# First batch row: Prelus, exponentials and conversion steps put ahead of the turns, and the second turn copy of every unit on ScalarE

## The chip, the core and the metric

The kernel runs on one core of one Trainium2 chip. A core has five engines, each with an instruction stream of its own: TensorE (PE, matmuls and transposes through it), VectorE (DVE), ScalarE (ACT), GpSimd (POOL) and SyncE (SP, which here issues DMA transfers). They meet at semaphores. Matmul results land in PSUM[...].

The metric is device microseconds of one execution. Before the change three runs gave 1376.87, 1380.67 and 1382.66 us; the median is **1380.67 us**. The profiled execution has a span of 1375.1 us, and all times within the span below are counted from its start.

## What is computed

Attention in which only the scores near the row's maximum survive, and then an MLP mixer over tokens and channels. All data are float32; the four MLP weights arrive as float64, and the kernel itself turns them into float32.

```python
# q, k, v: (8 batches, 8 heads, 576 tokens, 64)
scores = q @ k.transpose(0, 1, 3, 2) / 8
thresh = scores.max(-1, keepdims=True) - tau
scores = np.where(scores >= thresh, scores, -1e9)
attn   = np.exp(scores - scores.max(-1, keepdims=True))
attn   = attn / (attn.sum(-1, keepdims=True) + 1e-9)
x      = (attn @ v) as (8, 576, 512)

h   = np.maximum(x.transpose(0, 2, 1) @ w_tok1, 0) @ w_tok2     # over tokens
u   = x + h.transpose(0, 2, 1)
out = u + np.maximum(u @ w_ch1, 0) @ w_ch2                      # over channels
```

## The kernel before

The work of a batch row is cut into 18 units: two pairs of head pairs, nine units each; a unit is 128 query tokens of two heads, which are called h = 0 and 1. Units 0 to 17 are batch row 0. In this row no MLP work is there yet to fill gaps, and the exponentials are transposed by TensorE, through PSUM; this is a "turn". In later rows VectorE and DMA transpose them, and MLP steps are filled in between. The weights are converted from float64 from the start on, in small steps, three to a piece; 31 pieces in all.

The order in which the code emits instructions is the order in which each engine gets its own. The loop, for the first row:

```python
for u in range(len(units) + LAG + 4):            # LAG = 2
    ...
    w = u - LAG
    if on:
        scores(u)
    last = False
    if due and not in_blocks(due[0][1]):
        last = values_due(u)                     # values matmuls, after every third turn
    if 0 < u <= len(units):
        norm(u - 1)
    if b_now:
        weight(2)
    else:
        weight_to(2.25 * (u - 1.5))              # conversion steps, first part
    while copies:
        copies.popleft()()                       # xT <- pv, VectorE (L420)
    ...
    if back:
        wb, wp, wt = units[w]
        if not in_blocks(wb):
            for i in range(3):
                turn(w, i)                       # the turns of the unit two back
        ...
    if b_now:
        weight(2)
    if on:
        weigh(u)                                 # Prelus and exponentials
    ...
    if b_now:
        weight(2)
    elif u == 0:
        ...
    else:
        weight_to(2.25 * (u - 1))                # conversion steps, second part
    ...
        if t == 2:
            prep(n + 1)                          # q, k transposes on VectorE (L284)
        if t == 7 and n + 2 < len(pairs):
            prep(n + 2)
```

What a unit does, with the line numbers that the profile uses:

```python
def scores(u):
    sc = [(ps_3rd if b == 0 and (2 * u + h) % 3 == 2 else ps_sc).tile([P, 2, MAIN], ...) for h in range(2)]
    ...
        nc.tensor.matmul(sc[h][rows, f, 0:HS], lhsT=qT[r, cols], rhs=kT[...], ...)          # L302
    for h in range(2):
        nc.vector.tensor_reduce(out=mx[:, c], in_=sc[h][:, :, 0:HS], op=ALU.max, ...)       # L307
        nc.gpsimd.tensor_scalar(out=bias[:, c], in0=mx[:, c], scalar1=toff, ...)            # L308

def weigh(u):
    for h in range(2):
        nc.scalar.activation(out=eh, in_=sc[h][:, :, 0:HS], func=AF.Prelu, bias=..., ...)   # L317
    ...
    for h in range(2):
        nc.scalar.activation(out=eh, in_=eh, func=AF.Exp, accum_out=rs[:, h : h + 1], ...)  # L324

def norm(u):
    nc.vector.tensor_scalar(out=rr, in0=rs, ...)                                            # L331
    nc.vector.reciprocal(out=rr, in_=rr)                                                    # L332
    for h in range(2):
        nc.gpsimd.tensor_scalar(out=eh, in0=eh, scalar1=rr[:, h : h + 1], ...)              # L335

def turn(u, third):
    ...
    ps = ps_tr.tile([P, MAIN], F32, tag="tr", ...)          # two buffers, shared with the values matmuls
    for c in range(3):
        nc.tensor.transpose(out=ps[:, c, :], in_=e[:, k0 : k0 + P], identity=ident)         # L353
    on = nc.scalar.copy if third == 1 and u % 2 else nc.vector.tensor_copy
    on(out=eTs[key][...], in_=ps)                                                           # L355
```

`turn` is called with u two units back, so the ScalarE copies of odd units fall into odd units of the loop. The score tiles of the first row have three buffers, two to a unit: with the first Prelu of a unit the buffer comes free that the next unit's second score tile needs.

A conversion step k belongs to piece k // 3; each emits one VectorE instruction and, by its part, GpSimd's last instruction of the piece before with the load of a later piece, or one ScalarE instruction of the next piece:

```python
def weight(n):
    for k in range(steps_done, min(steps_done + n, 3 * len(pieces) + 1)):
        i, part = divmod(k, 3)
        if part == 0:
            on_gpsimd(i - 1)                     # L215
            if i:
                load_piece(i - 1 + NRAW)         # NRAW = 4 raw buffers
        else:
            on_scalar(i + 1, part - 1)           # L191, L193
        on_vector(i, part)                       # L201, L205, L209
        steps_done = k + 1

def weight_to(x):
    weight(max(int(x) - steps_done, 0))
```

Of the kernel before, what the change touches and what calls it, by code (L numbers as in the profile page):

```python
# [21 lines left out]
def kernel(  # L22
# [25 lines left out]
    nc = tc.nc  # L48
# [174 lines left out]
    def weight(n):  # L223

        nonlocal steps_done
# [5 lines that stand above are left out]
                    load_piece(i - 1 + NRAW)  # L231
            else:
                on_scalar(i + 1, part - 1)
            on_vector(i, part)
# [5 lines that stand above are left out]
# [36 lines left out]
    def in_blocks(b):  # L276
        return b > 0
# [10 lines left out]
    def scores(u):  # L288
        b, p0, t = units[u]
        sc = [  # L290
            (ps_3rd if b == 0 and (2 * u + h) % 3 == 2 else ps_sc).tile([P, 2, MAIN], F32, tag="sc", name=f"sc{h}_{u}") for h in range(2)
        ]
        if t == SHARED:
            parts = [(b * NP + p0, slice(MAIN, S), slice(0, 64)), (b * NP + p0 + 1, slice(0, LAST), slice(64, P))]
        else:
            o = P * t if t < SHARED else LAST + P * (t - SHARED - 1)
            parts = [(b * NP + p0 + (t > SHARED), slice(o, o + P), slice(0, P))]
        order = [(f, part, h) for f in range(2) for part in parts for h in range(2)]
        for f, (n, cols, rows), h in order if b else sorted(order, key=lambda o: o[2]):
            r = slice(D * h, D * h + D)  # L300
            qT, kT = heads[n]
            nc.tensor.matmul(sc[h][rows, f, 0:HS], lhsT=qT[r, cols], rhs=kT[r, HS * f : HS * f + HS], start=True, stop=True)  # L302
        mx = small.tile([P, 2], F32, tag="mx", name=f"mx_{u}")
        bias = small.tile([P, 2], F32, tag="bias", name=f"bias_{u}")
        for h in range(2):
            c = slice(h, h + 1)
            nc.vector.tensor_reduce(out=mx[:, c], in_=sc[h][:, :, 0:HS], axis=AX.XY, op=ALU.max)  # L307
            nc.gpsimd.tensor_scalar(out=bias[:, c], in0=mx[:, c], scalar1=toff, scalar2=-SCALE, op0=ALU.add, op1=ALU.mult)  # L308
        st[u] = sc, bias

    def weigh(u):
        sc, bias = st.pop(u)
        rs = small.tile([P, 2], F32, tag="rs", name=f"rs_{u}")
        e = work.tile([P, 2 * S], F32, tag="e", bufs=3, name=f"e_{u}")
        for h in range(2):
            eh = e[:, S * h : S * h + S].rearrange("p (f x) -> p f x", f=2)
            nc.scalar.activation(out=eh, in_=sc[h][:, :, 0:HS], func=AF.Prelu, bias=bias[:, h : h + 1], scale=SCALE, alpha=STEEP)  # L317
        st[u] = e, rs

        if b_now:  # L320
            fill(0.2)
        for h in range(2):
            eh = e[:, S * h : S * h + S]
            nc.scalar.activation(out=eh, in_=eh, func=AF.Exp, bias=ntau, accum_out=rs[:, h : h + 1])  # L324
            if b_now:
                fill(0.2)

    def norm(u):
        e, rs = st[u]
        rr = small.tile([P, 2], F32, tag="rr", name=f"rr_{u}")  # L330
        nc.vector.tensor_scalar(out=rr, in0=rs, scalar1=1e-9, scalar2=None, op0=ALU.add)  # L331
        nc.vector.reciprocal(out=rr, in_=rr)  # L332
        for h in range(2):
            eh = e[:, S * h : S * h + S]
            nc.gpsimd.tensor_scalar(out=eh, in0=eh, scalar1=rr[:, h : h + 1], scalar2=1.0, op0=ALU.mult, op1=ALU.mult)  # L335
        st[u] = e
# [3 lines left out]
    def turn(u, third):  # L340

        b, p0, t = units[u]
        key, place = (b, p0, t // GU), t % GU
        e = st[u]

        if third == 0 and place == 0:
            eTs[key] = work.tile([P, NK, GU * P], F32, tag="T", name=f"eT_{u}")
        if third == 2:
            st.pop(u)
        ps = ps_tr.tile([P, MAIN], F32, tag="tr", name=f"tr{third}_{u}")[:, 0 : 3 * P].rearrange("p (c x) -> p c x", c=3)  # L350
        for c in range(3):
            k0 = (3 * third + c) * P
            nc.tensor.transpose(out=ps[:, c, :], in_=e[:, k0 : k0 + P], identity=ident)  # L353
        on = nc.scalar.copy if third == 1 and u % 2 else nc.vector.tensor_copy
        on(out=eTs[key][:, 3 * third : 3 * third + 3, P * place : P * place + P], in_=ps)  # L355

    def turn_blocks(u):
# [149 lines left out]
    def fill(share):  # L507
        nonlocal credit
        credit += share * quota
        while todo and credit > 0:  # L510
            cost, step = todo.popleft()
            credit -= cost
            step()
        if not todo:
            credit = 0.0

    def push(b):
        nonlocal quota
        uT = xTs[b]
        steps, old = token_mlp(b), list(todo)  # L520
        todo.clear()

        for i, step in enumerate(steps):
            n = 2 if i in (NT, NT + NTK) else 1
            todo.extend(old[:n] + [step])
            del old[:n]
        todo.extend(old)
        for i in range(2) if b % 2 == 0 else range(2, (2 * S + GR - 1) // GR):
            todo.extend(channel_mlp(b - b % 2, uT, i))
        quota = (sum(c for c, _ in todo) - (KEEP if b else KEEP_FIRST)) / (UB - 1)  # L530
# [3 lines left out]
    b_now = 0  # L534
    LAG = 2

    def values_due(u):
        while due and due[0][0] <= u:
            _, b, p0, g = due.popleft()
            values(b, p0, g)  # L540
            if p0 == NP - 2 and g == 2:
                if not in_blocks(b):
                    return True
                push(b)
        return False

    for u in range(len(units) + LAG + 4):
        on = u < len(units)
        if u == UB:
            late.close()  # L550
            ps_mm = ctx.enter_context(tc.tile_pool(name="ps_mm", bufs=2, space=bass.MemoryType.PSUM))
        if on:
            b_now, p0, t = units[u]
            n = b_now * NP + p0
        w = u - LAG
        back = 0 <= w < len(units)
# [5 lines that stand above are left out]
            last = values_due(u)  # L562
# [3 lines that stand above are left out]
            weight(2)  # L566
        else:

            weight_to(2.25 * (u - 1.5))
        while copies:  # L570
            copies.popleft()()
        if last:
            push(0)
# [4 lines that stand above are left out]
                    turn(w, i)  # L578
            if wt % GU == GU - 1:
                g = wt // GU  # L580
                if g < 2:
                    split_middle(wb * NP + wp + g)
                due.append((u + (2 if in_blocks(wb) else 1), wb, wp, g))
        if b_now:
            fill(0.4)
        if back and in_blocks(wb):
            turn_blocks(w)
        if b_now:
            weight(2)
        if on:  # L590
            weigh(u)
        elif b_now:
            fill(0.6)
        if b_now:
            weight(2)
        elif u == 0:
            on_scalar(0, 0)
            on_scalar(0, 1)
        else:
            weight_to(2.25 * (u - 1))  # L600
        if on:


            when = {3: (2, 0, 2), 4: (2, 2, 4), 5: (2, 4, 6), 6: (2, 6, 8), 8: (3, 0, 3), 0: (1, 3, 6), 1: (1, 6, 8)}
            if u == 0:
                load_qk(1, (nc.sync, nc.sync), range(0, 3))
            if t in when:
                m, lo, hi = when[t]
                if n + m < len(pairs):
                    load_qk(n + m, (nc.scalar if b_now else nc.sync,) * 2, range(lo, hi))  # L610
            if t in (3, 7) and n + 2 + t // 4 < len(pairs):
                load_v(n + 2 + t // 4)
            if t == 2:
                prep(n + 1)
            if t == 7 and n + 2 < len(pairs):
                prep(n + 2)
        if due and in_blocks(due[0][1]):
            values_due(u)
# [31 lines left out]
```

## Time and profile before

| engine | busy, us | share of the span | instructions |
|---|---|---|---|
| TensorE (PE) | 1322.7 | 96% | 6226 |
| VectorE (DVE) | 588.2 | 43% | 1017 |
| ScalarE (ACT) | 581.8 | 42% | 1288 |
| GpSimd (POOL) | 356.0 | 26% | 683 |

A row of the timeline reads: start in us, duration in us, engine, source line, operation, output tile <- input tiles, shapes, how many instructions are merged in the row, and in brackets how long the engine stood idle before it and what ended that wait. "q" behind an engine's name is its instruction queue, PEld the weight loads of TensorE. L302 is line 302 of the kernel. A row of the waits reads: who waited <- for whom: total us, times, longest us. In the table of slices each digit is the busy share of one fortieth of the span in tenths (9 is 90% or more), and PEclk the clock that TensorE was granted, in tenths of full speed.

### The profile page before, as it was taken

The numbers are of one execution on the slowest core, as the hardware profiler recorded it, in microseconds if no ns is written. First come the engines' busy times: TensorE is split into PE (matmuls) and PEld (weight loads), VectorE is DVE, ScalarE is ACT, GpSimd is POOL, SyncE is SP. The second block draws the span as 40 slices with busy tenths as digits, with TensorE's granted clock in tenths as the row PEclk, the third lists the DMA queues.
The fourth block names the chain that finished last, engine by engine and source line by source line (L and its number), as shares of the span: only waits on it lengthen the run. The fifth ranks groups of instructions, "written<-read, shape, count | busy, mean of one in ns | idle before, by whom it ended". The sixth has DMA issues, their size and how long they took to land.

```text
span 1375.1 us, 17691 instructions
## 1 busy us (share of the span) xinstructions
PE 1322.7 (96%) x6226; PEld 817.9 (59%) x6226; DVE 588.2 (43%) x1017; ACT 581.8 (42%) x1288; POOL 356.0 (26%) x683
## 2 busy tenths in 40 slices
PE   6877799999999999999999999999999999999998
PEld 3444465646565666565665567565656576575675
DVE  6788875445444443434244444434333453201000
ACT  5666654454445444443434444353333444120110
POOL 4555653222222222222122222222121222100000
PEclk9988999999999999999999999999999999999999
DMA  5434655454544354433344435434433442400000
GB/s 121 98 96 125 183 142 124 100 123 98 122 109 114 82 121 94 113 88 95 77 100 94 113 77 123 106 83 98 103 87 75 107 103 63 115 1 16 8 11 21
DMA packets 278871, 128.20 MB, mean 93 GB/s; under 512 B 200896, under 2 KB 271552, under 8 KB 278784
## 3 DMA queue, kind: packets, MB, share of 16 engines
q1 hardware_dynamic: 150176, 111.06, 32.0%
q10 hardware_dynamic: 128608, 16.01, 7.3%
q8 instruction: 50, 0.82, 0.3%
q14 instruction: 37, 0.30, 0.1%
HBM read 43.25 MB, written 9.44 MB: 38 GB/s over the span
## 4 chain that ended last, share of the span: by engine, by line
PE 85%; DVE 7%; DMA 2%; SPq 2%; ACT 1%; issue 1%; POOL 1%; ACTq 0%; DVEq 0%; POOLq 0%
PE c L486 26%; PE c L470 26%; PE sc L302 11%; PE pv L413 9%; PE t L441 5%; PE t L448 3%; PE pv L408 3%; DVE mx L307 2%; SPq L374 2%; PE tx L432 1%; PE c L482 1%; DMA eT<-T 1%; PE tr L353 1%; DVE wc L205 1%; ACT e L317 1%
## 5 line engine op out<-in xcount | busy, mean ns | idle before, releaser
L307 DVE TENSOR_REDUCE mx<-sc 128x1 f32<-128x576 f32 x288 | 204.5, 751 | 487.9 <-PE sc L302 487.5
L470 PE MATMUL c<-xT,wc 128*128 128x256 f32 (+1 forms) x1920 | 399.4, 362 | 2.1 <-DVE xT L452 1.2
L486 PE MATMUL c<-wc,g 128*128 128x512 f32 x864 | 390.5, 597 | 0.0
L470 PEld LDWEIGHTS c<-xT,wc 128*128 128x128 f32 x1920 | 334.5, 191 | 71.5 <-issue 27.6
L308 POOL TENSOR_SCALAR bias<-mx,toff 128x1 f32<-128x1 f32 x288 | 82.8, 288 | 799.3 <-DVE mx L307 742.3
L317 ACT ACTIVATE e<-sc,bias 128x576 f32<-128x576 f32 x288 | 199.6, 739 | 162.0 <-POOL bias L308 161.4
L486 PEld LDWEIGHTS c<-wc,g 128*128 128x128 f32 x864 | 157.8, 190 | 175.7 <-issue 174.0
L471 ACT ACTIVATE g<-c 128x256 f32<-128x256 f32 (+1 forms) x240 | 86.7, 362 | 334.1 <-PE c L470 317.9
L324 ACT ACTIVATE e<-e,ntau 128x576 f32<-128x576 f32 x288 | 220.7, 771 | 0.0
L335 POOL TENSOR_SCALAR e<-e,rr 128x576 f32<-128x576 f32 x288 | 215.6, 761 | 15.8 <-DVE rr L332 4.3
L302 PE MATMUL sc<-kT,qT 64*128 64x288 f32 (+1 forms) x1280 | 196.6, 447 | 11.1 <-DVE kT L284 7.1
L365 DVE STREAM_TRANSPOSE T<-e 128x1152 f32<-128x1152 f32 x126 | 172.1, 1366 | 6.3 <-DMA eT<-T 2.6
L302 PEld LDWEIGHTS sc<-kT,qT 64*128 64x128 f32 (+1 forms) x1280 | 107.4, 184 | 98.3 <-issue 59.1
L413 PE MATMUL pv<-eT,lv 128*64 128x384 f32 (+1 forms) x1024 | 136.8, 409 | 0.0
L413 PEld LDWEIGHTS pv<-eT,lv 128*64 128x64 f32 x1024 | 76.1, 138 | 51.0 <-issue 43.6
L491 DVE COPY o<-c 128x512 f32<-128x512 f32 x36 | 24.9, 692 | 177.5 <-PE c L486 177.5
L418 ACT COPY xT<-pv 128x384 f32<-128x384 f32 (+1 forms) x56 | 21.0, 401 | 157.5 <-PE pv L413 157.5
L448 PE MATMUL t<-w,a 128*128 128x288 f32 x256 | 75.2, 421 | 7.2 <-DVE xT L452 5.3
L441 PE MATMUL t<-x_sb,w 128*128 128x512 f32 x160 | 72.1, 598 | 0.0
L448 PEld LDWEIGHTS t<-w,a 128*128 128x128 f32 x256 | 45.6, 191 | 32.2 <-issue 11.4
L452 DVE TENSOR_TENSOR xT<-xT,t 128x288 f32<-128x288 f32 x64 | 28.2, 446 | 80.5 <-PE t L448 80.0
L324 ACT ACTIVATION_READ_ACCUMULATOR e<-e,ntau 128x1 f32 x288 | 56.5, 196 | 0.0
(44 smaller groups left out, 554.7 us busy)
## 6 DMA issues: line engine op xcount, KB each, us to landing
eT<-T SPq DMA_DIRECT2D x672, 108.0 KB, 2.2
scratch<-in_moe_w_ch_dram SPq DMA_DIRECT2D x24, 512.0 KB, 3.7
lv<-in_v_dram SPq DMA_DIRECT2D x32, 288.0 KB, 3.3
out_dram<-o SPq DMA_DIRECT2D x36, 256.0 KB, 2.2
lk<-in_k_dram ACTq DMA_DIRECT2D x111, 72.0 KB, 2.6
lq<-in_q_dram ACTq DMA_DIRECT2D x106, 72.0 KB, 2.3
lq<-in_q_dram SPq DMA_DIRECT2D x22, 72.0 KB, 3.2
lk<-in_k_dram SPq DMA_DIRECT2D x17, 72.0 KB, 3.3
```

The costliest lines, as they stand in the source:

```text
L302: nc.tensor.matmul(sc[h][rows, f, 0:HS], lhsT=qT[r, cols], rhs=kT[r, HS * f : HS * f + HS], start=True, stop=True)
L307: nc.vector.tensor_reduce(out=mx[:, c], in_=sc[h][:, :, 0:HS], axis=AX.XY, op=ALU.max)
L317: nc.scalar.activation(out=eh, in_=sc[h][:, :, 0:HS], func=AF.Prelu, bias=bias[:, h : h + 1], scale=SCALE, alpha=STEEP)
L324: nc.scalar.activation(out=eh, in_=eh, func=AF.Exp, bias=ntau, accum_out=rs[:, h : h + 1])
L335: nc.gpsimd.tensor_scalar(out=eh, in0=eh, scalar1=rr[:, h : h + 1], scalar2=1.0, op0=ALU.mult, op1=ALU.mult)
L365: nc.vector.transpose(out=T[:, :, place, :].rearrange("p a (c x) -> p c a x", c=NK), in_=e.rearrange("p (c a x) -> p c a x", c=NK, a=4))
L413: nc.tensor.matmul(to[r], lhsT=lv[:, j, :], rhs=e[j], start=False, stop=(c == NI - 1), skip_group_check=True)
L441: nc.tensor.matmul(ps, lhsT=w1[:, t, P * m : P * m + P], rhs=x_sb[:, t, :], start=(t == 0), stop=(t == NT - 1))
L448: nc.tensor.matmul(ps, lhsT=s["a"][:, m, P * c : P * c + P], rhs=w2[:, m, HS * f : HS * f + HS], start=(m == 0), stop=(m == NTK - 1))
L470: nc.tensor.matmul(ps, lhsT=wc1[:, j, c, :], rhs=uT[:, c, GR * i : GR * i + n], start=(c == 0), stop=(c == NCC - 1))
L471: nc.scalar.activation(out=s["g"][:, j, 0:n], in_=ps, func=AF.Relu)
L486: nc.tensor.matmul(flat, lhsT=s["g"][:, j, P * t : P * t + P], rhs=wc2[:, j, :], start=False, stop=(j == NJ - 1), skip_group_check=True)
```

## The change

Three things change, all of them for the first batch row. The second part of each turn is copied by ScalarE in every unit, not in odd ones alone, which takes work from VectorE. `weigh` is emitted ahead of the turns, so that ScalarE comes to a unit's Prelus and exponentials before it comes to a copy of a turn. And the two calls of `weight_to` become one, ahead of the turns, with as many steps at the unit's end as before.

```diff
@@ def turn(u, third)
-        on = nc.scalar.copy if third == 1 and u % 2 else nc.vector.tensor_copy
+        on = nc.scalar.copy if third == 1 else nc.vector.tensor_copy
@@ the loop over units, ahead of the copies and turns
-            weight_to(2.25 * (u - 1.5))
+            weight_to(2.25 * (u - 1))
+
+            if on:
+                weigh(u)
         while copies:
             copies.popleft()()
@@ behind the turns
-        if on:
+        if on and b_now:
             weigh(u)
         elif b_now:
             fill(0.6)
@@
         elif u == 0:
             on_scalar(0, 0)
             on_scalar(0, 1)
-        else:
-            weight_to(2.25 * (u - 1))
```

## The prediction

> **What bounds the kernel now.** I began with the page's table of slices (34.4 us each), to see where the one changed stretch lies.
>
> ```profile
> PE   6877799999999999999999999999999999999998
> ...
> DVE  6788875445444443434244444434333453201000
> ...
> PEclk9988999999999999999999999999999999999999
> ```
>
> From the sixth slice on TensorE is busy throughout at full clock, so what an earlier stretch gains or loses moves the end one for one. Only in the first four slices is VectorE (DVE) as busy as TensorE. The changed code acts on the first batch row, units 0 to 17, and its turns run on into units 18 and 19. Taking the start of a unit's first maximum (L307) as the unit's start, the timeline gives units 3 to 18 at 22.85, 26.78, 31.67, 39.70, 44.02, 48.98, 53.85, 58.45, 63.53, 71.48, 76.56, 82.27, 89.17, 93.14, 99.81 and 106.18 us. Those are 15 units in 83.3 us: 10 without values matmuls take 49.2 us (4.92 each), and 5 with them (5, 8, 11, 14, 17) take 34.1 us.
>
> Next, the timeline of unit 6, whose three turn copies are all on VectorE (rows of other engines left out):
>
> ```profile
> 39.70 1.42 DVE L307 TENSOR_REDUCE mx<-sc 128x1 f32<-128x576 f32 x2 [0.22 <-issue]
> ...
> 41.32 0.29 DVE L201 TENSOR_SCALAR w<-scratch 128x288 uint32<-128x288 uint32 x1
> ...
> 41.52 1.01 DVE L355 COPY eT<-tr 128x384 f32<-128x384 f32 x2
> ...
> 42.12 0.55 PE L353 MATMUL tr<-ident,e 128*128 128x128 f32 x3 [1.32 <-DVE eT L355]
> ...
> 42.60 1.25 PE L302 MATMUL sc<-kT,qT 64*128 64x288 f32 x8
> ...
> 42.71 0.56 DVE L355 COPY eT<-tr 128x384 f32<-128x384 f32 x1 [0.17 <-PE tr L353]
> ...
> 43.18 0.92 DVE L205 SCALAR_TENSOR_TENSOR w<-scratch,w 128x288 uint32<-128x288 uint32 x1
> ...
> 44.02 1.41 DVE L307 TENSOR_REDUCE mx<-sc 128x1 f32<-128x576 f32 x2
> ```
>
> There is a loop through two engines. TensorE does a unit's first two turn groups at once, but the third must wait until VectorE has copied one of them out (two "tr" buffers), and the next unit's scores stand behind that third group. VectorE hardly idles: while TensorE does the third group and the scores, it copies the second and third group and does one more conversion step (L205).
>
> In odd units ScalarE copies the second group. Unit 9:
>
> ```profile
> 54.60 0.48 ACT L355 COPY eT<-tr 128x384 f32<-128x384 f32 x1 [0.92 <-PE tr L353]
> ...
> 55.13 0.55 PE L353 MATMUL tr<-ident,e 128*128 128x128 f32 x3 [0.57 <-ACT eT L355]
> ```
>
> Here the third group goes 0.54 us before VectorE copies its first (55.67): it takes the buffer that ScalarE has freed, and waits for VectorE not at all.
>
> Last, the waits over 0 to 210 us (total, times, longest):
>
> ```profile
> ACT eT L355 <- PE tr L353: 23.2, 7, 6.1
> ...
> PE tr L353 <- DVE eT L355: 17.7, 8, 3.6
> ...
> DVE xT L420 <- PE pv L413: 7.7, 4, 2.9
> ```
>
> ScalarE stands 23.2 us before its turn copies, with the Prelus queued behind them. That looks like the thing to mend, but ScalarE is busy only 12 to 17 us of each 20 there.
>
> [...]in unit 5 ScalarE is idle 6.11 us before its copy at 37.60 and only then starts the Prelu at 37.97. So emission order matters.[...] the granted clock was 0.52 at 75 to 80 us and 0.66 at 95 to 100, and six transposes took 1.54 us where 0.88 is usual.[...] L205 on 288 columns took 0.92 us at 43.18, beside GpSimd's L215 at 43.05; 64x256 took 0.42 at 38.54 alone.
>
> **The change part by part.**
>
> 1. Nine copies of the second group (units 2, 4, ... 18) go from VectorE to ScalarE. Each adds about 0.5 us start to start on VectorE: 9 × 0.5 = 4.5 us of VectorE time. ScalarE gets 9 × 0.48 us, beside other work.
>
> 2. Prelus and exponentials go ahead of the turns. A Prelu no longer waits for a turn copy. The gain is where it held the next scores: the eight matmuls of unit 6, behind unit 5's late Prelu, took 2.05 us instead of 1.25. The price is that the ScalarE copy now comes after the exponentials. Counted from the unit's first maximum: maxima and the second bias 2.0, second Prelu 0.7, exponentials 1.6, so the copy runs from about 4.3 to 4.8. The build's waits show the consequence: the third group of every unit up to 15 now waits for VectorE, also in odd units.
>
> 3. All conversion steps (2 or 3 a unit) come ahead of the copies. They no longer lie under TensorE's third group and scores, but on the loop. From the rows above the loop becomes: two maxima and the reciprocal 1.61 (58.45 to L201 at 60.06 in unit 10); the steps W; first copy to third group 0.60 (41.52 to 42.12); third group to scores 0.48; scores to the next maximum 1.34 (52.51 to 53.85, where the maximum waited for the scores). That is 4.03 us + W. A step costs start to start 0.20 (L201), 0.40 (L205), 0.36 (L209) at 288 columns, and 0.35, 0.60, 0.60 at 512. From the start of the first copy VectorE then has 2.42 us until the next maximum and only two copies to do in it, the second from 1.19 to 1.74: about 0.7 us idle on either side of it.
>
> The steps that each unit gets, by the built order, give W; I add 0.2 us a unit for GpSimd's lock (the blocked steps of before lost some 4.4 us in 18 units). Unit 12 gets 0.45 more, for 16 short score matmuls (1.8 us). The q and k transposes in 7 and 16 (1.42 us) find 0.7 us idle and add 0.75.
>
> Units 3, 4, 6, 7, 9, 10, 12, 13, 15, 16 were 3.93, 4.89, 4.32, 4.96, 4.60, 5.08, 5.08, 5.71, 3.97, 6.67, sum 49.2. With W of 0.95, 1.2, 0.6, 0.56, 0.96, 0.6, 1.2, 1.55, 0.95, 1.2 they become 5.2, 5.4, 4.8, 5.5, 5.2, 4.8, 5.9, 5.8, 5.2, 6.2, sum 54.0 at full clock. Two of the ten at half clock, 1.0 us each for the longer third group and scores, make 56.0: **6.8 us lost**. The 4.5 us of part 1 is already inside this: it shortens VectorE's work, which no longer sets the loop.
>
> Units with values: TensorE's 3.7 to 4.7 us of pv set these, before and after, and the conversions lie under that wait (xT waited 2.85 us in unit 5). Unit 5 gains 1.0 (early Prelu, no step between the last copy and the maximum), 11 gains 0.25, 14 gains 0.55, 17 gains 0.7; unit 8, where pv was early and two steps now precede the xT copy, loses 0.3: **2.2 us won**. Unit 18's copy on ScalarE: 0.4 won. Units 0 to 2: nothing.
>
> Sum: +6.8 − 2.2 − 0.4 = +4.2 us, 1380.7 → 1384.9.
>
> **The rivals.** (a) VectorE's work is the bound, as its 96 to 99% in 25-30, 40-50 and 90-95 us suggests. Then the nine copies and shorter lock conflicts (4.5 + about 2) come off, with the 2.2 and 0.4: some 9 us, 1372. Against it: its filler is what moves. (b) ScalarE becomes the bound: conversions 0.9, Prelus 1.35, exponentials 1.6, copy 0.48 make 4.3 us a unit, below 4.9; but where its late copy still holds a buffer (the first group of the next unit waits for it, as built), a slip would add 0.5 us to some units: 1387. (c) Clock: if TensorE's wait for the first copy, now about 1.9 us in every unit instead of 1.3 to 3.0 in even ones,[...] three half-clock units fewer save 3 to 4 us, and it comes out even at 1380; if less often, 1388.
>
> **Range and chances.** The table rests on differences of tenths of a microsecond, and (a) and (c) both pull down, so I take 1383.0. Three runs of before differ by 5.8 us, as much as the effect: 1374 to 1391 should hold it 8 times in 10. A change of 2% is 27.6 us, nearly a third of the 83 us, and nothing here is so large: faster 0.015, same 0.97, slower 0.015.
>
> **What would show it.** Right: VectorE idle 0.5 to 0.7 us before the third-group copy and before the maximum in nearly every unit without values; ScalarE's wait before its copies far below 23.2 us; units of 4.8 to 6.2 us without values and 6.4 with; unit 18 starting about 4 us later than 106.18, and the rest shifted by that. Wrong: unit 18 starting at 98 to 102 us, the maxima of the next unit ready before VectorE is, or, against the one-for-one shift, a first row and an end that move by different amounts because the weight transfers of 140 to 195 us run at their own pace.

## The result and the profile after

The changed kernel takes **1390.32 us** in the median of six runs (1387.92 to 1394.34); the kernel before, run beside it, takes 1381.87 us (1376.87 to 1382.66). The ratio is **1.0069, with a 95% interval of 1.0048 to 1.0091**: some 9.5 us longer by this ratio (the two medians are 8.5 us apart). The time lies just inside the range that I gave. The size of the loss does not fit: I predicted 1383.0, a loss of 2 us, where the working itself had come to 4.2.

The table of slices of the changed kernel:

```profile
PE   5777799999999999999999999999999999999998
...
DVE  5668885454444444434333444433443453201000
...
PEclk7887999999999999999999999999999999999999
```

Only the first four slices differ in kind: TensorE and VectorE are both less busy, and the clock that TensorE is granted there is lower. Unit 18 starts at 119.43 us instead of 106.18, and from there to the end the two kernels stay 11.8 to 13.5 us apart: nothing is won or lost later. (Spans are 1387.1 and 1375.1 us. The runs of before, with those beside the experiments, spread from 1376.9 to 1386.5 us, and the profiled one took 1376.9, so the two traces are further apart than the medians.)

From here on, the **row length** is the time from the first maximum of unit 3 to that of unit 18; it leaves out the start of the span, after which unit 3 begins anywhere from 22.76 to 25.02 us from run to run. Busy times over just this stretch, before (us from start to end of the stretch: its length, then busy time and instructions of TensorE, its weight loads, VectorE, ScalarE and GpSimd, granted clock, DMA share, GB/s):

```profile
22.85:106.18 83.33, 66.54 (x411) 40.10 (x409) 68.34 (x146) 54.91 (x115) 48.74 (x79) 0.90 0.39 92
```

and after:

```profile
23.52:119.43 95.91, 69.48 (x413) 40.63 (x414) 64.12 (x138) 61.76 (x128) 53.69 (x79) 0.82 0.34 79
```

VectorE was indeed relieved (68.3 to 64.1 us), but the stretch is 12.6 us longer, so VectorE idles 31.8 us of it instead of 15.0. TensorE has the same work and takes 3 us more for it (69.5 for 66.5), at a granted clock of 0.82 for 0.90.

What it now waits for shows in the timeline of unit 9, an odd one, in the changed kernel:

```profile
60.38 1.42 DVE L307 TENSOR_REDUCE mx<-sc 128x1 f32<-128x576 f32 x2 [0.68 <-PE sc L302]
...
62.00 0.29 DVE L201 TENSOR_SCALAR w<-scratch 128x288 uint32<-128x288 uint32 x1
...
62.32 0.47 DVE L205 SCALAR_TENSOR_TENSOR w<-scratch,w 128x288 uint32<-128x288 uint32 x1
62.83 0.80 DVE L209 SCALAR_TENSOR_TENSOR w<-h,w 128x288 f32<-128x288 f32 x1
...
63.55 0.55 DVE L355 COPY eT<-tr 128x384 f32<-128x384 f32 x1
...
64.15 0.55 PE L353 MATMUL tr<-ident,e 128*128 128x128 f32 x3 [3.05 <-DVE eT L355]
...
64.52 0.46 ACT L355 COPY eT<-tr 128x384 f32<-128x384 f32 x1
...
64.63 1.57 PE L302 MATMUL sc<-kT,qT 64*128 64x288 f32 x8
64.73 0.56 DVE L355 COPY eT<-tr 128x384 f32<-128x384 f32 x1 [0.64 <-PE tr L353]
...
66.28 0.76 DVE L307 TENSOR_REDUCE mx<-sc 128x1 f32<-128x576 f32 x1 [0.99 <-PE sc L302]
```

Before, ScalarE copied this unit's second group out of PSUM 0.75 us after the first maximum began (54.60 against 53.85), and TensorE's third group followed at 1.28 us. Now ScalarE comes to the copy at 4.14 us, behind the Prelus and exponentials; the third group waits for VectorE's first copy, behind three conversion steps, and starts at 3.77 us. TensorE has stood still for 3.05 us by then, and its scores take 1.57 us where 1.25 is the quick value. VectorE idles 0.64 us before the third group's copy and 0.99 us before the next maximum.

The waits over the same stretch, after:

```profile
ACT e L317 <- POOL bias L308: 28.6, 23, 3.5
...
PE tr L353 <- DVE eT L355: 25.1, 10, 3.6
DVE mx L307 <- PE sc L302: 13.4, 14, 1.7
DVE eT L355 <- PE tr L353: 11.3, 15, 1.0
...
ACT eT L355 <- PE tr L353: 5.4, 4, 1.8
```

Before these were 5.2, 11.4, 1.7, 4.0 and 23.2 us. ScalarE's wait before its copies, which the change set out to mend, is down to 5.4 us; it now waits for the biases of the next unit instead (28.6 us). TensorE and VectorE wait for each other.

### The profile page after: what moved, and what is told of

It reads as the page before. It is cut to its first block, busy times and chain, and to the rows that moved or that the text cites. A ratio compares the mean times of both kernels' runs of the same rounds, so it can differ in the third digit from the quotient of the medians.

```text
span 1387.1 us, 17688 instructions
## 1 busy us (share of the span) xinstructions
PE 1324.0 (95%) x6226; PEld 815.9 (59%) x6226; DVE 584.1 (42%) x1008; ACT 587.2 (42%) x1297; POOL 361.7 (26%) x683
## 4 chain that ended last, share of the span: by engine, by line
PE 88%; DVE 6%; DMA 2%; SPq 1%; ACT 1%; issue 1%; ACTq 0%; POOL 0%; DVEq 0%; POOLq 0%
PE c L486 27%; PE c L470 26%; PE sc L302 12%; PE pv L413 9%; PE t L441 5%; PE t L448 3%; PE pv L408 3%; DVE mx L307 2%; SPq L374 1%; PE tx L432 1%; PE c L482 1%; PE tr L353 1%; DVE wc L205 1%; DMA eT<-T 1%; DVE wc L209 1%
## 5 line engine op out<-in xcount | busy, mean ns | idle before, releaser
L335 POOL TENSOR_SCALAR e<-e,rr 128x576 f32<-128x576 f32 x288 | 222.5, 785 | 15.7 <-DVE rr L332 4.6
L302 PEld LDWEIGHTS sc<-kT,qT 64*128 64x128 f32 (+1 forms) x1280 | 104.6, 183 | 100.1 <-issue 60.6
L448 PEld LDWEIGHTS t<-w,a 128*128 128x128 f32 x256 | 45.8, 192 | 32.0 <-issue 11.4
L353 PE MATMUL tr<-ident,e 128*128 128x128 f32 x162 | 31.7, 331 | 33.8 <-DVE eT L355 31.9
```

What stands on the lines that cost most here:

```text
L448: nc.tensor.matmul(ps, lhsT=s["a"][:, m, P * c : P * c + P], rhs=w2[:, m, HS * f : HS * f + HS], start=(m == 0), stop=(m == NTK - 1))
```

## The experiments

Three things change at once, so I ran each of them alone and in pairs. Four theories go by letters in the expectations. **A**: what costs is that the ScalarE copy comes late; the third group then depends on VectorE, and each step ahead of VectorE's first copy lengthens the loop. **B**: the steps ahead of the copies cost by themselves. **C**: either ScalarE's load, in the first experiment, or, further down, TensorE's half clock (0.50 granted, as in unit 4 there). **D**: the late copy holds buffers, and the place of the steps is secondary. All ratios are to the kernel before on the same chip. Row lengths are from one profile each, and several microseconds in the total go from run to run, so the ratios decide.

**The copies alone.** In the kernel before:

```diff
-        on = nc.scalar.copy if third == 1 and u % 2 else nc.vector.tensor_copy
+        on = nc.scalar.copy if third == 1 else nc.vector.tensor_copy
```

> Before, with the second turn copy of every unit on ScalarE and nothing else changed (Prelus behind the turns, steps in two parts). Theory A, that the late ScalarE copy is what costs: here the copy stands ahead of the Prelus, so the third group is released by ScalarE early in even units too, and VectorE is relieved of 9 copies; unit 18 starts at 100 to 103 us (before 106.2, after 119.4) and the whole is 3 to 6 us shorter than before. Theory B, that the conversion steps ahead of the copies cost: this kernel does not have them, unit 18 at 101 to 105. Theory C, that ScalarE is overloaded by the copies: unit 18 at 108 to 112.

Measured: 1373.99 us, ratio **0.9956 (0.9929 to 0.9984)**; row length 80.37 us, unit 18 at 103.36. Faster than either kernel, as A said, though unit 18 came 0.4 us later than A's latest. B's 101 to 105 us holds as well, so this run speaks only against C, an overloaded ScalarE. The timeline of its unit 10, an even one:

```profile
57.67 1.41 DVE L307 TENSOR_REDUCE mx<-sc 128x1 f32<-128x576 f32 x2
...
58.39 0.49 ACT L355 COPY eT<-tr 128x384 f32<-128x384 f32 x1
...
58.81 1.57 ACT L317 ACTIVATE e<-sc,bias 128x576 f32<-128x576 f32 x2
...
58.93 0.55 PE L353 MATMUL tr<-ident,e 128*128 128x128 f32 x3 [1.16 <-ACT eT L355]
...
59.47 1.01 DVE L355 COPY eT<-tr 128x384 f32<-128x384 f32 x2
...
60.40 0.94 DVE L205 SCALAR_TENSOR_TENSOR w<-scratch,w 128x288 uint32<-128x288 uint32 x1
```

The ScalarE copy stands in front of the Prelus, and those would have had to wait for the bias anyway (58.78). The third group starts 1.26 us after the maximum, before VectorE has copied anything, and VectorE runs through this unit without a gap. The granted clock over the row is 0.97. ScalarE still waits 22.2 us before its copies, almost as long as before: the kernel became faster without that wait getting smaller.

**The Prelus and exponentials alone.** In the kernel before:

```diff
             weight_to(2.25 * (u - 1.5))
+            if on:
+                weigh(u)
 ...
-        if on:
+        if on and b_now:
             weigh(u)
```

> Before, with Prelus and exponentials ahead of the turns and nothing else changed (copies of odd units alone on ScalarE, steps in two parts). Theory A, that the late ScalarE copy costs: the third group of odd units, which ScalarE released early, now waits for VectorE; unit 18 at 109 to 112 us, 3 to 6 us longer than before. Theory B, the steps ahead of the copies: they are not moved, so unit 18 at 104 to 107, as before or a little better for the earlier Prelus.

Measured: 1383.67 us, ratio 1.0016 (0.9982 to 1.0049); row length 90.95 us, unit 18 at 113.88. The trace lies on A's side (7.6 us longer), the ratio, some 2 us, is within noise of no change. Undecided by itself.

**The conversion steps alone.** In the kernel before:

```diff
-            weight_to(2.25 * (u - 1.5))
+            weight_to(2.25 * (u - 1))
 ...
-        else:
-            weight_to(2.25 * (u - 1))
```

> Before, with all conversion steps ahead of the copies and nothing else changed. Theory A, the late ScalarE copy: odd units keep their early third group, only even units have the steps on the loop; unit 18 at 107 to 110 us, 1 to 4 us longer. Theory B, the steps ahead of the copies cost by themselves: unit 18 at 113 to 118, most of the 13 us.

Measured: 1381.92 us, ratio 1.0013 (0.9986 to 1.0039); row length 88.86 us, unit 18 at 112.54. Between the two expectations in the trace, near A's in the ratio.

**Copies and steps**, that is, the changed kernel with `weigh(u)` back behind the turns.

```diff
-            if on:
-                weigh(u)
 ...
-        if on and b_now:
+        if on:
             weigh(u)
```

> The changed kernel with Prelus and exponentials put back behind the turns: all second copies on ScalarE, all steps ahead of the copies. Theory A: ScalarE releases the third group early in every unit, so the steps lie beside TensorE's work; unit 18 at 101 to 105 us, 1 to 5 us shorter than before, although it has two of the three parts of the change. Theory B: the steps are still ahead of the copies, unit 18 at 113 to 118 us.

Measured: 1376.15 us, ratio **0.9970 (0.9944 to 0.9995)**; row length 81.77 us, unit 18 at 104.53. This is what decides between A and B. All steps lie ahead of the copies, exactly as in the changed kernel, and yet it is faster than before, because ScalarE releases the third group early in every unit. Its waits show it: 10.3 us of TensorE's third groups for ScalarE's copy in ten waits, and none for VectorE's. With the other two parts in place, moving the Prelus ahead makes 1.0069 out of 0.9970: 13.7 us. B falls.

**Copies and Prelus**, that is, the changed kernel with the steps back in two parts.

```diff
-            weight_to(2.25 * (u - 1))
+            weight_to(2.25 * (u - 1.5))
 ...
+        else:
+            weight_to(2.25 * (u - 1))
```

> The changed kernel with the conversion steps put back into two parts, one ahead of the copies and one behind. Theory A (the ScalarE copy comes after the exponentials, so the third group waits for VectorE's first copy, and every step ahead of that copy lies on the loop): half of the steps leave the loop; unit 18 at 110 to 115 us (before 106.2, after 119.4, with the copies alone 103.4, with the Prelus alone 113.9). Theory B (the steps by themselves): 103 to 107 us.

Measured: 1381.56 us, ratio 0.9998 (0.9972 to 1.0025); row length 88.68 us, unit 18 at 111.53, as A said. With the copy late, moving the second part of the steps ahead of VectorE's first copy is worth 1.0069 − 0.9998, about 10 us; with the copy early it was worth 0.9970 − 0.9956, 2 us within noise.

**Prelus and steps**, that is, the changed kernel with the copies of even units back on VectorE.

```diff
-        on = nc.scalar.copy if third == 1 else nc.vector.tensor_copy
+        on = nc.scalar.copy if third == 1 and u % 2 else nc.vector.tensor_copy
```

> The changed kernel with the ScalarE copies of even units given back to VectorE. Theory A: with the copy behind the exponentials, it makes little difference to the third group who copies the second one; VectorE has nine more copies, which fall into its idle time or lie ahead of the third group's copy; unit 18 at 117 to 123 us. If the nine copies on ScalarE are themselves a part of the loss: 112 to 116 us.

Measured: 1392.12 us, ratio 1.0075 (1.0051 to 1.0099); row length 97.37 us, unit 18 at 121.94. As A said: when the copy is late, who makes it hardly matters, and the nine copies go into or out of VectorE's idle time. Alone they were worth 6 us (0.9956).

The eight combinations:

| copies all on ScalarE | Prelus ahead | steps ahead | row length, us | ratio |
|---|---|---|---|---|
| no | no | no | 83.33 | 1 |
| yes | no | no | 80.37 | 0.9956 |
| no | yes | no | 90.95 | 1.0016 |
| no | no | yes | 88.86 | 1.0013 |
| yes | no | yes | 81.77 | 0.9970 |
| yes | yes | no | 88.68 | 0.9998 |
| no | yes | yes | 97.37 | 1.0075 |
| yes | yes | yes | 95.91 | 1.0069 |

The parts don't add. Prelus and steps cost about 2 us each alone, which is within noise of nothing, and 10 together (1.0075).

**All steps behind the copies**, with the rest of the change kept.

```diff
-            weight_to(2.25 * (u - 1))
             if on:
                 weigh(u)
 ...
+        else:
+            weight_to(2.25 * (u - 1))
```

> The changed kernel with all conversion steps behind the turn copies instead of ahead of them; Prelus and exponentials stay ahead of the turns and the ScalarE copy stays late. Theory A: the steps leave the loop and lie beside TensorE's third group and scores; unit 18 at 105 to 110 us. Theory D, that the late ScalarE copy itself holds buffers and the place of the steps is secondary: 114 to 119 us.

Measured: 1378.45 us, ratio 0.9973 (0.9939 to 1.0007); row length 85.48 us, unit 18 at 108.47. As A said, and against D: the copy is as late as in the changed kernel, yet taking the steps off the loop brings back 0.0096, some 13 us. So the late copy by itself is no more the loss than the steps by themselves: with either of the two taken back the loss is gone (0.9970 and 0.9973).

**Only the exponentials behind the turns**: ScalarE does Prelus, turn copy, exponentials. The loop over h with `AF.Exp` leaves `weigh` for a function `exps`, called for the first row where `weigh` used to stand.

```diff
             if on:
                 weigh(u)                 # Prelus alone in the first row
 ...
+        if on and not b_now:
+            exps(u)
         if on and b_now:
             weigh(u)
```

> The changed kernel with only the exponentials put back behind the turns: ScalarE does a unit's Prelus, then the turn copy, then the exponentials. Theory A: the copy comes some 1.6 us earlier and releases the third group, which no longer waits for VectorE; unit 18 at 103 to 108 us. If even the Prelus ahead of the copy make it too late, 111 to 117.

Measured: 1389.88 us, ratio 1.0056 (1.0028 to 1.0084); row length 96.00 us, unit 18 at 119.44. My main expectation, 103 to 108, was wrong; the other branch was the right one, and still too hopeful. The wait of this kernel:

```profile
PE tr L357 <- ACT eT L359: 24.5, 10, 3.4
```

The third group now waits for ScalarE (L359 is its turn copy), 24.5 us in 10 waits, as long as it waited for VectorE in the changed kernel (25.1, 10). In unit 9 the copy starts 2.6 us after the maximum (63.45 against 60.83), 1.5 us sooner than in the changed kernel, and the third group starts at 3.15 us instead of 3.77. In unit 7 it starts later, at 3.30 instead of 2.79, although VectorE's first copy had ended at 2.73: in this trace the third group does not take whichever buffer is copied out first. Over the ten units without values matmuls it starts 3.37 us after the maximum on the mean, in this kernel as in the changed one. So it is not enough to put the exponentials behind the copy. It has to stand ahead of the Prelus, which themselves wait for maximum and bias.

**TensorE kept warm**, that is, busy where it would wait. The changed kernel, with the transposes of the second group done three times, the same result written again, in units without values matmuls:

```diff
-        for c in range(3):
+        for c in [0, 1, 2] * (3 if third == 1 and place else 1):
             k0 = (3 * third + c) * P
```

> The changed kernel with the three transposes of the second group done three times over in units without values matmuls (the same result written again, six more transposes a unit in TensorE's wait). Theory C, that the longer waits mainly cost by TensorE's half clock (granted 0.82 over units 3 to 17, 0.90 before): the granted clock rises to 0.93 or more and unit 18 comes at 109 to 114 us. Theory A without the clock: the third group waits for VectorE as long as it did, and unit 18 stays at 116 to 120 us; the difference between 119.4 and this run is the clock's share.

Measured: 1381.98 us, ratio **1.0005 (0.9974 to 1.0036)**; unit 18 at 111.33. Row:

```profile
23.79:111.33 87.54, 65.18 (x473) 41.96 (x474) 64.04 (x137) 61.82 (x128) 54.00 (x79) 0.96 0.36 87
```

and wait:

```profile
PE tr L353 <- DVE eT L355: 19.6, 10, 3.0
```

With more work TensorE is busy for less time (65.2 us for 69.5), at a granted clock of 0.96 for 0.82, and the kernel is 0.0064, some 9 us, shorter, although the third group still waits 19.6 us: as C expected. Unit 4 shows where the time goes. In the changed kernel its third group starts 3.54 us after the first maximum, and TensorE works at a granted clock of 0.50:

```profile
32.25 0.90 PE L353 MATMUL tr<-ident,e 128*128 128x128 f32 x3 [2.06 <-DVE eT L355]
33.08 2.30 PE L302 MATMUL sc<-kT,qT 64*128 64x288 f32 x8
```

Kept warm, the third group starts at 3.55 us, no sooner, but it takes 0.55 us and the scores 1.25, as in unit 6 of the changed kernel (46.00 to 47.60 us) at a granted clock of 1.00:

```profile
32.19 0.55 PE L353 MATMUL tr<-ident,e 128*128 128x128 f32 x3 [1.77 <-DVE eT L355]
32.67 1.25 PE L302 MATMUL sc<-kT,qT 64*128 64x288 f32 x8
```

The half clock is a cost of the first order here. What remains, the kernel before pays in part too, hence the control:

**The kernel before kept warm**, in its even units without values matmuls:

```diff
-        for c in range(3):
+        for c in [0, 1, 2] * (3 if third == 1 and place and u % 2 == 0 else 1):
             k0 = (3 * third + c) * P
```

> Before, with the second group's transposes done three times over in its even units without values matmuls (odd units have no long wait for VectorE). Control for the changed kernel kept warm, whose unit 18 came at 111.3 us against 119.4. If the half clock is a cost that the change brought (theory C): before has little of it (granted 0.90), unit 18 at 104 to 106 us, and of the 13.2 us between the two kernels 6 to 8 are the clock's. If it costs both alike: unit 18 at 98 to 101 us, and the change's loss is 10 to 13 us at full clock too.

Measured: 1377.02 us, ratio 0.9968 (0.9943 to 0.9993); unit 18 at 106.08, but from a start of unit 3 that came 2.2 us late; row:

```profile
25.02:106.08 81.06, 64.96 (x445) 43.58 (x444) 69.01 (x145) 55.68 (x117) 49.96 (x79) 0.97 0.40 94
```

Both expectations counted from the start of the span and were upset by that late start (without it unit 18 would have come at 103.9, between the two); row lengths and ratios are free of it. Before gains 0.0032 by being kept warm, the changed kernel 0.0064. So of the 0.0069 between them about half (1.0005 against 0.9968: 0.0037, some 5 us) is left when both are warm, and about half is clock that the change loses. By row lengths it is 6.5 us of 12.6 that stay. The intervals are 0.005 to 0.006 wide. What the changed kernel gains by being kept warm is clear of them; the 0.0037 that stays is not, so "about half" is all that can be said. Even kept warm, the third group of unit 13 took 0.90 us, as it did in the changed kernel at a granted clock of 0.50 (90.24 to 93.30 us), so the clock's share may be larger.

**GpSimd's lock.** This stands for what the kernel before shows: L205 over 288 columns took 0.44 us at 50.54, where no L215 ran, and 0.92 us at 43.18, beside GpSimd's L215 (from 43.05). The changed kernel with the steps ahead of the reciprocal, so that GpSimd's normalisations come after them:

```diff
+        if on and not b_now:
+            weight_to(2.25 * (u - 1))
         if 0 < u <= len(units):
             norm(u - 1)
 ...
-            weight_to(2.25 * (u - 1))
```

> The changed kernel with the conversion steps put ahead of the reciprocal instead of behind it, so that GpSimd's two normalisations cannot start until the steps are through. If GpSimd's lock on the steps is a large part of the loss: the steps fall to 0.2-0.6 us each and unit 18 comes at 113 to 117 us (changed kernel 119.4). If it is small, as in the prediction's 0.2 us a unit: 117 to 120 us.

Measured: 1393.83 us, ratio 1.0085 (1.0057 to 1.0113); row length 99.41 us. Neither expectation: unit 18 came at 123.86, and the row is 3.5 us longer than in the changed kernel; in the ratios the two are within noise of each other. From its groups on VectorE over the row (busy us, mean ns | idle before):

```profile
L209 DVE SCALAR_TENSOR_TENSOR wc<-h,wc 128x512 f32<-128x512 f32 x5 | 5.3, 1052 | 0.4
...
L331 DVE TENSOR_SCALAR rr<-rs 128x2 f32<-128x2 f32 x15 | 4.6, 309 | 0.0
```

and the same groups in the changed kernel:

```profile
L209 DVE SCALAR_TENSOR_TENSOR wc<-h,wc 128x512 f32<-128x512 f32 x5 | 4.2, 835 | 0.1
...
L331 DVE TENSOR_SCALAR rr<-rs 128x2 f32<-128x2 f32 x15 | 2.4, 157 | 0.0
```

The 512-column L201 and L205 took the same in both (about 0.42 and 0.69 us), so the normalisations had hardly held them up. In this order GpSimd's L215 starts where VectorE does the next L209 or L331, and there it holds them: 2.2 us in all on an operation over two columns, and 1.1 us on these five L209. The overlap with GpSimd was moved, not removed, so this run does not say what the changed kernel would be without it. How small it is there is read from the trace, under part 3 below.

**Copies on ScalarE, all steps behind**, meant to be the fastest. In the kernel before, with the line of the first experiment and:

```diff
-        else:
-            weight_to(2.25 * (u - 1.5))      # the first part; the second stays
```

> A version meant to be faster than both: before, with every second copy on ScalarE ahead of the Prelus, and all conversion steps behind the turn copies. Theory A: with the third group released by ScalarE, VectorE's work is the bound and the place of the steps matters little, as in copies alone (unit 18 at 103.4, ratio 0.9956) and copies with all steps ahead (104.5, 0.9970): unit 18 at 100 to 104 us, ratio 0.993 to 0.997. If steps ahead of the copies still cost something, 99 to 101 us.

Measured: 1375.61 us, ratio **0.9955 (0.9935 to 0.9976)**; row length 82.02 us, unit 18 at 105.51. In ratio the same as the copies alone, as expected; in the trace a little longer than expected. With the copy early the place of the steps can't be told apart by these runs. This version and the copies alone beat the kernel before by 0.4% and the changed one by 1.1%.

## Why the prediction was right or wrong

**That an earlier stretch moves the end one for one**: right, to about a microsecond. The 13.25 us at unit 18 were 12.0 at the end. (VectorE is as busy as TensorE in the fifth slice too, not in the first four alone; that one lies behind the first row.)

**Part 1, nine copies off VectorE**: right in size (4.2 us less busy) and right that they would bring nothing behind the exponentials (1.0069 with them, 1.0075 without). I missed what the same copies do where they stand ahead of the Prelus: early in every unit they release the third group, and are worth 6 us.

**Part 2, the late ScalarE copy, the third group depending on VectorE in odd units**: right. 4.3 us after the maximum was the estimate, 4.14 in unit 9. It is one half of the cause: without it the other two parts together are a gain (0.9970). The other half is part 3: with the copy late but the steps behind it, there is no loss either (0.9973).

**Part 3, the steps on the loop**: right. The first copy came 1.61 us + W + lock after the maximum, where W and the lock were to sum to 11.8 us over the ten units without values matmuls. From the trace (first copy's start less the unit's start, less 1.61) it was 11.6, so GpSimd's lock is the small term there that I had. Full-clock sum of the ten units: 54.0 predicted, **54.2 us in the changed kernel kept warm**, where unit 13 still lost 1.4 us with its third group at 0.90 us; without that it would be 52.8. The loop itself was therefore sized well, rather too large than too small. (Two terms in it were too large: the 0.45 us for unit 12's short matmuls was not there, and the q and k transposes added 0.6 us, not 0.75.)

**The step that failed is "Two of the ten at half clock, 1.0 us each"**: the clock's term of the sum was mis-sized. In the changed kernel the ten units took 59.8 us, kept warm 54.2: 5.5 us for the clock where I had 2.0. From first copy to next maximum I had 2.42 us; it was 2.42 to 2.73 in units 3, 6, 9 and 15, but 3.73 to 3.82 in 4, 10, 12 and 13, and 3.71 in 16, where it includes the q and k transposes. Kept warm, the same piece took 2.35, 2.42 and 2.38 us in units 4, 10 and 12, and 3.01 in 16. So it was five of ten units, four of them at 1.3 to 1.4 us each, and not two at 1.0. In the same five the third group took 0.79 to 0.90 us, in the other five 0.55; from its start to the end of the scores the granted clock was 0.50 in units 4, 10, 12 and 13 and 0.53 in 16, and 0.77 to 1.00 in the others. I had taken the share of half-clock units over from the kernel before, where it took 0.90 in units 13 and 16 (granted clock 0.50), though each of the ten now has a wait of 1.5 to 3.6 us in TensorE, which my rival (c) even mentions. The granted clock was 0.90 before and 0.82 after. VectorE's idle time on either side of the third group's copy, which I had put at 0.5 to 0.7 us, was that in the quick units (0.64 and 0.68 us in unit 6) and more in the slow ones (0.99 and 1.66 in unit 4).

**"Units with values ... 2.2 us won"**: wrong in sign, and as large a miss as that of the ten units (4.2 us against 3.7). They took 36.2 us instead of 34.1: 7.66, 7.36, 6.82, 7.62 and 6.70. The largest part is unit 8, 7.36 for 4.87. In the kernel before its values matmuls (pv) had begun 1.74 us ahead of its first maximum (47.24 against 48.98), because unit 7's third group had been released by ScalarE; in the changed kernel 0.31 us ahead (52.71 against 53.02). I saw that release in odd units and did not follow it into the unit after. Kept warm, the five take 33.3 us and unit 8 takes 5.73: here, too, 2.8 us go with the clock (in the changed kernel 0.50 was granted at the head of unit 8, from 53.02 to 55.00 us), for which I had nothing, and what stays is still 1.4 us more than the 31.9 I had.

**The rivals**: (a), that VectorE is the bound, is not true of this kernel, in which it idles 31.8 us of the row, and shading the number toward it took 2 us off a working that was too low already. (b), ScalarE as the bound, is not supported: it stood waiting for the biases for 28.6 us, and the waits of the row show none of TensorE for its late copy. (c) named the quantity that went wrong, the granted clock; its upper branch, 1388, was for more units at half clock.

Not settled: how much of the loss is clock to better than "half"; and the row lengths of the Prelus and of the steps alone, 7.6 and 5.5 us longer, against ratios of only 2 us with intervals that would allow anything from 2 us shorter to 7 us longer.

## What to carry to other kernels

An engine that waits at the head of its queue is not a loss by itself: here ScalarE's 23 us before the turn copies were what kept the copies early, and those fed TensorE. Before an instruction is moved ahead of a waiting one, ask who waits for the one that is passed. The longer wait of TensorE counted twice here: once for itself, and once for the slower clock behind it (0.82 granted over the row, 0.96 once the waits were partly filled), which was about half of the loss.

## What the runs showed of the hardware that I had not expected

Six extra transposes in each unit without values matmuls, of no use for the result, made the changed kernel some 9 us faster and raised the granted clock from 0.82 to 0.96. Transposes, merely repeated, were enough for that. Three of them took 0.90 us at a granted clock of 0.50 (units 4, 10, 12 and 13 of the changed kernel) and 0.55 us at 1.00 (units 6 and 15).

GpSimd's two-input L215 held up even VectorE's L331, which reads and writes two columns: 309 ns in the mean instead of 157 once the two stood next to each other. Twelve of the fifteen still took 0.15 to 0.16 us; the three that began while L215 ran took 0.70, 0.77 and 1.26 us and ended as it did. Here a small instruction was not safe beside a long one on GpSimd.
